# Late attention tiles on one Trainium2 core: pairing a tile's scores with the values' product of its second last tile

## The chip, the cores and the metric

The kernel runs as one program on one core of a Trainium2 chip. The metric is device time in microseconds (us), median of several runs. One more execution was recorded by the profiler; all rows below come from it.

## The reference

```python
# attention in chunks of 32 queries; context: 16 keys left, 8 right, and 8 memory keys
scores = scale * np.matmul(q_c, k_full.transpose(0, 1, 3, 2))
scores = scores - np.max(scores, axis=-1, keepdims=True)
a = np.exp(scores)
a = a / (np.sum(a, axis=-1, keepdims=True) + 1e-09)
out[:, :, c_start:c_end] = np.matmul(a, v_full)      # (4, 8, 768, 64)
...
gate = 1.0 / (1.0 + np.exp(-(x @ w_gate)))           # x: 3072 x 512, d_ff 1536
x = (gate * (x @ w_val)) @ w_out
h = x @ w_in                                         # d_ff 2048
out = (h * (1.0 / (1.0 + np.exp(-1.702 * h)))) @ w_out
```

## The kernel before

The 3072 tokens are 32 attention tiles of 96 tokens, and 6 blocks of 512 tokens for the two gated networks. Each operand of a network's product is split into a high and a low part, so that a product is three matrix products.

**Early and late tiles.** Nine tiles are done early: TensorE transposes for them. The other 23, the late tiles (numbered 0 to 22 here, in the order of their work), run between the products of the first network's blocks. Block b's products (`first_product`, L771 and L778, then the gate, L795 to L806, then `gemm2`, L962) share the engines with the attention tiles of block b+1. A late tile goes through these steps:

- SyncE (SP) loads queries, keys, memory keys and values by many small DMAs, all through one helper (L323): 12 for the queries, 16 to 20 for the keys of two tiles, 2 or 3 for the values. SP issues one after the other. Queries have two buffers (`f`), keys two (`raw`), values one (`vn`).
- VectorE (DVE) turns queries (`ev_q`, L498, into `qt`) and keys (`ev_k`, L506, into `kt`) in 32 x 32 blocks. `qt` and `kt` have one buffer each.
- TensorE (PE) makes the scores (`pe_s`, L521), in the two PSUM banks that are `bank_70` and `bank_71`.
- DVE takes the maximum (L538), subtracts it (L541); ScalarE (ACT) takes exp (L549); DVE sums (L578), adds 1e-9 and inverts (L580, L581).
- The norm (L589) multiplies by the inverse, into `pn` (the buffer is `raw_78` in the rows): 56 key columns of all 96 rows on GpSimd (POOL), and the 8 memory columns on DVE, in two instructions of 64 and 32 rows.
- DVE turns the result (`ev_pt`, L643, eight instructions, into `pt`, one buffer).
- PE multiplies with the values (`pe_pv`, L668), in the same two banks.
- ACT and DVE evict the banks to `xh` and `xl` (L713, L716). Tokens of the last two blocks go another way: ACT evicts to `qt` (L691), and SP stores `qt` to `x_dram` by L323. The next `ev_q` writes `qt` and has to wait for that store. Of the late tiles, 7 to 10 and 16 to 22 have such tokens.

**Bursts.** On PE a late tile's scores are one burst with the values' product of the tile before it: first `pe_pv` of tile n-1, then `pe_s` of tile n. So between two bursts a tile goes through its whole chain, from the maximum to `pt`.

**Other work in these stretches.** `park` (L996) adds the two parts of 24 weights on GpSimd into two staging buffers, and SP stores them to `wf_dram` by L323; a third park waits for the first one's store.

**The order** is made by a list scheduler (`Schedule`): every step is added with an engine, a planned duration, what it reads and writes, and for products a due time. A step's due time is the earliest of its followers', less its duration, a latency and a slack. Each engine takes, of its steps that are ready in planned time, the one due first. The order is fixed when the program is built: each engine works through its list in that order, and waits where an input is not there. A DMA costs 0.45 us of SP in the plan:

```python
add("sp", 0.45, lambda: nc.sync.dma_start(out=dst(), in_=src), r=list(r), w=[key], nbytes=n)
```

Of the kernel before, what the change touches and what calls it, by code (L numbers as in the profile page):

```python
# [123 lines left out]
def c_dve(n, k=1):  # L124
    return k * 0.13 + n / 960.0
# [11 lines left out]
def kernel(  # L137
# [221 lines left out]
    def attention(t, bufs, banks, pe_path, extra=None, last=False):  # L359
# [6 lines left out]
        kk = bufs.k  # L366
        T = bufs.t

        def tadd(eng, dur, fn, r=(), w=(), **kw):
            add(eng, dur, fn, r=r, w=w, slack=SL, **kw)  # L370

        def load_ctx(name, src, mem):

# [60 lines left out]
        else:  # L434
# [78 lines left out]
            tadd("dve", c_dve(2 * 384), ev_k, r=kkb, w=[(kk["kt"], 0), (kk["kt"], 1)])  # L513
# [42 lines left out]
        if pe_path:  # L556
            tadd("pe", 0.75, pe_s, r=rs, w=[kb0, kb1], margin=mg)
        else:

            held = late.pop() if late else None  # L560

            def pe_burst():
                if held:
                    held[0]()
                pe_s()

            tadd("pe", 1.6, pe_burst, r=rs + (held[1] if held else []), w=[kb0, kb1])
            if held:
                held[2]()
            load_ctx("vn", v, mem_v)  # L570
        for hp, kb in enumerate((kb0, kb1)):
            tadd("dve", 0.34 + edge, lambda hp=hp: ev_max(hp), r=[kb], w=[(kk["mx"], hp)])
        for hp, kb in enumerate((kb0, kb1)):
            tadd("dve", 0.34, lambda hp=hp: ev_sub(hp), r=[kb, (kk["mx"], hp)], w=[(kk["e"], hp)])
        ke = [(kk["e"], 0), (kk["e"], 1)]
        tadd("act", c_act(512), ev_exp, w=ke)
        tadd(
# [15 lines left out]
        if pe_path:  # L593

            def ev_norm(c):
                r = (c * CH, (c + 1) * CH)
                eng = nc.vector if en[c] == "dve" else nc.gpsimd
                norm(eng, T["pw"][r[0] : r[1], :, c * CH : c * CH + CTX], r, (0, CTX))

            def ev_norm_m():  # L600
                norm(nc.vector if en[0] == "dve" else nc.gpsimd, T["pw"][:, :, TK:P], (0, TQ), (CTX, KW))

            en = ["pool", "pool", "pool"] if t in (0, 2) else ["dve", "pool", "pool"]
            for c in range(NCK):
                tadd(en[c], 0.75 if en[c] == "dve" else 1.2, lambda c=c: ev_norm(c), r=ke + [kk["sm"]], w=[(kk["pw"], c)])
            tadd(en[0], 0.25 if en[0] == "dve" else 0.35, ev_norm_m, r=ke + [kk["sm"]], w=[(kk["pw"], 3)])

            def pe_pt():
                for h in range(H):
                    a, p = divmod(h, NP)  # L610
                    nc.tensor.transpose(
                        bt[a][:, p * TQ : (p + 1) * TQ], T["pw"][:, h, :], ident()[:TQ, :TQ]
                    )

            def ev_pt(a):
                src = bt[a][:, : NP * TQ]
                dst = T["pt"].rearrange("p (a h) s -> p a (h s)", a=2)[:, a, :]
                nc.scalar.activation(dst, src, AF.Copy)

            tadd("pe", 0.7, pe_pt, r=[(kk["pw"], c) for c in range(4)] + [bufs.kid], w=kbt, margin=mg)  # L620
            for a in range(2):
                tadd("act", c_act(384), lambda a=a: ev_pt(a), r=[kbt[a]], w=[(kk["pt"], a)])
        else:

            def ev_norm():
                norm(nc.vector, T["pn"][0:L, :, 3 * CH - NM : 3 * CH], (0, L), (CTX, KW))
                norm(nc.vector, T["pn"][L:TQ, :, CTX:KW], (L, TQ), (CTX, KW))

            tadd(
                "pool",  # L630
                0.95,
                lambda: norm(nc.gpsimd, T["pn"][:, :, 0:CTX], (0, TQ), (0, CTX)),
                r=ke + [kk["sm"]],
                w=[(kk["pn"], 0)],
            )
            tadd("dve", c_dve(128, 2), ev_norm, r=ke + [kk["sm"]], w=[(kk["pn"], 1)])
# [87 lines left out]
        if pe_path:  # L724
            tadd("pe", 0.8, pe_pv, r=rp, w=[kbv], margin=mg)
            if t < NPRO - 1 or t >= NPRO:
                evict()
            else:

                evict(0)  # L730
                held_back.append(lambda: evict(1))
        else:
            late.append((pe_pv, rp, evict))
            if last:
                tadd("pe", 0.9, pe_pv, r=rp, w=[kb0, kb1])
# [440 lines left out]
    def x_prep(b, mark=None, src=y_dram, b0=0, rk=lambda m, bb: [("y", m, bb)]):  # L1176
        for k in range(2):
            tk = 4 + k
            for i, (m, bb) in enumerate(((k, b), (k, b + 1), (2 + k, b), (2 + k, b + 1))):

                def load(i=i, m=m, bb=bb):
                    c = slice((bb - b0) * BLK, (bb - b0 + 1) * BLK)
                    nc.sync.dma_start(out=ys[i], in_=src[m * P : (m + 1) * P, c])

                add("sp", 0.45, load, r=rk(m, bb) + ([mark] if mark else []), w=[KYS[i]], nbytes=P * BLK * 4)

            def sub(o, x, y):
                def fn():
# [363 lines left out]
```

## Time and profile before

| | us |
|---|---|
| median of 3 runs | 1183.88 |
| lowest, highest | 1183.59, 1184.81 |
| profiled execution, its own time | 1182.71 |
| its span, first to last instruction | 1180.7 |

In the profile an engine's busy time counts its instructions on data; instructions that issue a DMA or wait for a semaphore are not counted. `[4.71 <-DMA f<-in_q_dram]` behind a row says that the engine was idle for 4.71 us ahead of it, and that the landing of a DMA from `in_q_dram` to `f` ended that. PE stands idle for few microseconds of its span; it slows down where its clock is granted at the lower of two levels (1.2 instead of 2.4 GHz).

### The profile page before, as it was taken

Reading aid. Unit: us, or ns where it says so; the run is one execution under the profiler, and the core shown is the slowest. Engines: PE = TensorE matmul, PEld = TensorE weight load, DVE = VectorE, ACT = ScalarE, POOL = GpSimd, SP = SyncE. Lnnn points to the kernel's source line nnn. Section 1 sums busy time; section 2 is a strip of 40 time slices with the busy share of each in tenths; the row PEclk is TensorE's granted clock in tenths of the full one; section 3 lists DMA queues with packets and bytes.
Section 4 is the critical chain, followed back from the end, with each engine's and each line's share of the span. In section 5 each row is a group of like instructions: output and inputs, shape, how many; then the busy total and the mean of one; then the engine's idle time right before and its main releaser. Section 6 shows DMA issues by size and latency. Waiting matters only on the chain.

```text
span 1180.7 us, 19478 instructions
## 1 busy us (share of the span) xinstructions
PE 1152.8 (98%) x7288; PEld 961.2 (81%) x7288; DVE 797.8 (68%) x1506; ACT 529.9 (45%) x953; POOL 114.5 (10%) x104
## 2 busy tenths in 40 slices
PE   8899999999989999999999999999999999999998
PEld 7788898997778788888888888888888888888887
DVE  7899668887878567888786978878343356243442
ACT  6778522223212222476554767755233344243332
POOL 5333313011122000000000000000000000000000
PEclk9899999999999999999999999999999999999999
DMA  9766244335344421533436555675243443244100
GB/s 210 221 186 187 74 108 106 55 60 130 67 89 102 98 55 38 174 117 108 150 118 227 181 164 182 205 219 160 67 123 105 121 149 115 63 127 125 35 36 36
DMA packets 211069, 144.39 MB, mean 122 GB/s; under 512 B 146208, under 2 KB 166944, under 8 KB 210976
## 3 DMA queue, kind: packets, MB, share of 16 engines
q1 hardware_dynamic: 207520, 136.87, 41.5%
q10 hardware_dynamic: 3456, 6.29, 1.4%
q8 instruction: 57, 0.93, 0.3%
q14 instruction: 36, 0.29, 0.1%
HBM read 107.45 MB, written 35.65 MB: 121 GB/s over the span
## 4 chain that ended last, share of the span: by engine, by line
PE 82%; SPq 6%; DVE 5%; DMA 3%; issue 2%; ACT 1%; POOL 0%; DVEq 0%; ACTq 0%; POOLq 0%
PE bank L1306 29%; PE bank L745 22%; PE bank L962 13%; PE bank L771 10%; SPq L323 6%; PE bank L778 5%; DVE pt L643 1%; PE bank L668 1%; PE bank L521 1%; DVE raw L589 1%; DMA y_dram<-f 1%; DMA wf_dram<-f 1%; DMA raw<-in_moe_w_out_dram 1%; DVE pw L589 0%; DVE sm L578 0%
## 5 line engine op out<-in xcount | busy, mean ns | idle before, releaser
L1306 PE MATMUL bank<-sb_x,sb_r 128*128 128x512 f32 x1512 | 362.8, 389 | 0.7 <-ACT sb_s L1318 0.7
L1306 PEld LDWEIGHTS bank<-sb_x,sb_r 128*128 128x128 f32 x1512 | 283.6, 188 | 60.6 <-ACT sb_s L1318 1.8
L745 PE MATMUL bank<-w,gh 128*128 128x512 f32 x624 | 192.0, 389 | 0.0
L771 PE MATMUL bank<-xh,w 128*128 128x512 f32 (+1 forms) x464 | 161.2, 359 | 5.0 <-DVE sig L798 3.0
L771 PE MATMUL bank<-xl,w 128*128 128x512 f32 (+1 forms) x464 | 159.6, 355 | 0.0
L962 PE MATMUL bank<-gh,w 128*128 128x512 f32 (+1 forms) x656 | 157.3, 364 | 1.0 <-ACT f L982 1.0
L745 PEld LDWEIGHTS bank<-w,gh 128*128 128x128 f32 x624 | 117.1, 188 | 24.3
L962 PEld LDWEIGHTS bank<-gh,w 128*128 128x128 f32 x656 | 114.8, 189 | 21.3 <-ACT f L982 1.4
L1322 DVE TENSOR_TENSOR sb_s<-bank,sb_s 128x512 f32<-128x512 f32 x108 | 74.3, 690 | 73.7 <-PE bank L1306 61.8
L745 PE MATMUL bank<-w,gl 128*128 128x512 f32 x312 | 121.4, 389 | 0.0
L778 PE MATMUL bank<-xh,w 128*128 128x512 f32 (+1 forms) x464 | 109.0, 359 | 0.0
L1318 ACT ACTIVATE sb_s<-bank 128x512 f32<-128x512 f32 x108 | 65.1, 603 | 87.9 <-PE bank L1306 82.0
L771 PEld LDWEIGHTS bank<-xh,w 128*128 128x128 f32 x464 | 88.7, 191 | 19.4 <-DVE sig L798 3.8
L771 PEld LDWEIGHTS bank<-xl,w 128*128 128x128 f32 x464 | 88.7, 191 | 12.3
L778 PEld LDWEIGHTS bank<-xh,w 128*128 128x128 f32 x464 | 78.4, 190 | 12.9 <-issue 0.2
L803 ACT ACTIVATE gh<-sig 128x512 fp32r<-128x512 f32 (+1 forms) x58 | 32.3, 557 | 110.1 <-DVE sig L798 109.7
L643 DVE STREAM_TRANSPOSE pt<-raw 32x256 f32<-32x256 f32 x184 | 79.9, 434 | 2.3
L962 PE MATMUL bank<-gl,w 128*128 128x512 f32 (+1 forms) x328 | 80.3, 367 | 1.1 <-DVE gl L806 1.1
L1349 ACT ACTIVATE sig<-sb_s 128x512 f32<-128x512 f32 x72 | 45.3, 632 | 57.0 <-DVE sb_s L1322 36.0
L745 PEld LDWEIGHTS bank<-w,gl 128*128 128x128 f32 x312 | 58.6, 188 | 12.3
L795 ACT ACTIVATE sig<-bank 128x512 f32<-128x512 f32 (+1 forms) x58 | 30.6, 528 | 83.7 <-PE bank L778 74.7
L962 PEld LDWEIGHTS bank<-gl,w 128*128 128x128 f32 x328 | 56.8, 189 | 10.8 <-DVE gl L806 1.3
(162 smaller groups left out, 1480.9 us busy)
## 6 DMA issues: line engine op xcount, KB each, us to landing
sb_r<-wc_dram SPq DMA_DIRECT2D x133, 256.0 KB
raw<-in_moe_w_out_dram SPq DMA_DIRECT2D x24, 512.0 KB
raw<-in_moe_w_in_dram SPq DMA_DIRECT2D x16, 512.0 KB
wc_dram<-sb_r SPq DMA_DIRECT2D x15, 512.0 KB
wf_dram<-f SPq DMA_DIRECT2D x24, 256.0 KB
y_dram<-f ACTq DMA_DIRECT2D x24, 256.0 KB
raw<-wf_dram SPq DMA_DIRECT2D x24, 256.0 KB
out_dram<-f SPq DMA_DIRECT2D x23, 256.0 KB
```

The lines of the kernel that those rows point to most:

```text
L323: add("sp", 0.45, lambda: nc.sync.dma_start(out=dst(), in_=src), r=list(r), w=[key], nbytes=n)
L643: nc.vector.transpose(T["pt"][r * CH : (r + 1) * CH, :, c * CH : (c + 1) * CH], T["pn"][c * CH : (c + 1) * CH, :, kb * CH : (kb + 1) * CH],)
L745: nc.tensor.matmul(ps_out, a, c, start=(first and i == 0 and j == 0), stop=(last and i == n - 1 and j == 2),)
L771: nc.tensor.matmul(bank[bk][:, :n], w[:, 0, ts[t]], x[xb][:, t, c0 : c0 + n], start=t == 0 and x is xhs, stop=False)
L778: nc.tensor.matmul(bank[bk][:, :n], w[:, 1, ts[t]], xhs[xb][:, t, c0 : c0 + n], start=False, stop=t == NK - 1)
L795: nc.scalar.activation(sig[:, :n], bank[src_sig][:, :n], AF.Tanh, scale=scale / 2)
L803: nc.scalar.activation(gh[:, :n], sig[:, :n], AF.Copy, scale=0.5)
L962: nc.tensor.matmul(bank[into[m]][:, c0 : c0 + n], w[:, wi, m * P : (m + 1) * P], g[:, :n], start=f == 0 and j == 0 and c0 == 0, stop=f == ...
L1306: nc.tensor.matmul(bank[bk], w[:, o : o + P], xt[x, k][:, xl, :], start=first and k == 0 and wl == 0 and xl == 0, stop=k == 1 and wl == 1, ...
L1318: add("act", c_act(BLK), lambda: nc.scalar.activation(work[n], bank[bk], AF.Copy), r=[("bank", bk)], w=[n])
L1322: nc.vector.tensor_tensor(out=work[n], in0=bank[bk], in1=work[n], op=ALU.add)
L1349: add("act", c_act(BLK), lambda: nc.scalar.activation(sigs[i], src(), AF.Tanh, scale=0.851), r=[ksrc], w=[ks])
```

## The change

It touches the late tiles and numbers of the scheduler.

1. A burst pairs the scores of tile n with the values' product of tile n-2 (before: n-1). The list `late` holds two tiles; a tile's second half (`rest`: loading the values, norm, `ev_pt`) is added to the schedule after the burst of the next tile, since `vn`, `pn` and `pt` have one buffer each. After the last tile two tiles are finished one after the other.
2. GpSimd forms all norms: the two instructions for the memory columns move there from DVE.
3. Planned durations: `ev_k` 0.97 (before 0.93), maximum and subtraction 0.42 each (before 0.34), `ev_pt` 1.75 for each half (before 1.59), a burst 1.75 or 0.8 (before 1.6), and 13.3 ns (before 2.5 ns) on each product from block 1 on. A burst is due 4 us sooner, the first loads of `x_prep` 10 us sooner. SP's 0.45 us stays.

```diff
-            held = late.pop() if late else None
+            held = late.pop(0) if len(late) > 1 else None
...
                 if held:
-                    held[0]()
+                    held["pv"]()
                 pe_s()
-            tadd("pe", 1.6, pe_burst, r=rs + (held[1] if held else []), w=[kb0, kb1])
+            tadd("pe", 1.75 if held else 0.8, pe_burst, r=rs + (held["rp"] if held else []), w=[kb0, kb1], more=4.0)
             if held:
-                held[2]()
-            load_ctx("vn", v, mem_v)
+                held["evict"]()
+            for x in late:
+                x["rest"]()
+        d_sm = 0.34 if pe_path else 0.42
...
             def ev_norm():
-                norm(nc.vector, T["pn"][0:L, :, 3 * CH - NM : 3 * CH], (0, L), (CTX, KW))
-                norm(nc.vector, T["pn"][L:TQ, :, CTX:KW], (L, TQ), (CTX, KW))
+                norm(nc.gpsimd, T["pn"][0:L, :, 3 * CH - NM : 3 * CH], (0, L), (CTX, KW))
+                norm(nc.gpsimd, T["pn"][L:TQ, :, CTX:KW], (L, TQ), (CTX, KW))
...
+            def rest():
+                load_ctx("vn", v, mem_v)
                 tadd(
-                    "dve",
-                    c_dve(1024, 4),
-                    lambda part=part: ev_pt(part),
-                    r=[(kk["pn"], 0), (kk["pn"], 1)],
-                    w=[(kk["pt"], part)],
+                    "pool",
+                    0.95,
+                    lambda: norm(nc.gpsimd, T["pn"][:, :, 0:CTX], (0, TQ), (0, CTX)),
...
+                tadd("pool", 0.6, ev_norm, r=ke + [kk["sm"]], w=[(kk["pn"], 1)])
...
-            late.append((pe_pv, rp, evict))
+            late.append(dict(pv=pe_pv, rp=rp, evict=evict, rest=rest))
             if last:
-                tadd("pe", 0.9, pe_pv, r=rp, w=[kb0, kb1])
-                late.pop()[2]()
+                for x in list(late):
+                    if x is not late[0]:
+                        x["rest"]()
+                    tadd("pe", 0.9, x["pv"], r=x["rp"], w=[kb0, kb1])
+                    x["evict"]()
...
     for b in range(NB - 2):
         n = BLK
+        if b:
+            step_ns[0] = 32 / 2400.0
```

**SP, before: from the store of tile 16's last tokens to that of tile 17's.** The order counts SP's DMAs; the first row here is the 503rd from the first late tile's first query load on, the last one the 551st. `f_79` and `f_80` are the two query buffers, `raw_77` one of the two for keys.

```order
L323 DMA x_dram<-qt 128x4x64
L323 DMA f_79<-in_mem_k_dram 8x4x32 x4
L323 DMA f_79<-in_q_dram 32x4x32 x3
L323 DMA wf_dram<-f_82 128x512
L323 DMA f_79<-in_q_dram 32x4x32 x9
L323 DMA f_80<-in_q_dram 32x4x32 x12
L323 DMA raw_77<-in_k_dram 32x7x32 x16
L323 DMA vn<-in_v_dram 112x8x64
L323 DMA vn<-in_mem_v_dram 8x8x64
L323 DMA x_dram<-qt 128x4x96
```

**SP, with the change: the same two stores.** They are now the 526th and the 564th.

```order
L323 DMA x_dram<-qt 128x4x64
L323 DMA f_80<-in_q_dram 32x4x32 x5
L323 DMA raw_77<-in_k_dram 32x7x32 x12
L323 DMA wf_dram<-f_82 128x512
L323 DMA raw_77<-in_k_dram 32x7x32 x4
L323 DMA f_79<-in_q_dram 32x4x32 x12
L323 DMA vn<-in_v_dram 112x8x64
L323 DMA vn<-in_mem_v_dram 8x8x64
L323 DMA vn<-in_v_dram 8x8x64
L323 DMA x_dram<-qt 128x4x96
```

The loads of a tile's queries stand further ahead of these stores than before: with the change the queries of tile 21 come ahead of the second store, before they come behind it. Tile 17's store comes after burst 19 with the change (before: burst 18), and `ev_q` of tile 20 waits for it (before: of tile 19).

On PE, ahead of the scores of tile 20 with the change stand 1024 product instructions of 512 columns and 720 of 256; ahead of the scores of tile 18 before stand 1020 and 720. So the bursts of tile 18 before and of tile 20 with the change stand at the same place among the products, four instructions apart.

**DVE, before: from the maximum of tile 16 to the end of its `ev_pt`** (`xl` is the eviction, `sig` and `gl` the network's gate, `qt` and `kt` the next tile's).

```order
L538 TENSOR_REDUCE mx<-bank_70 96x4
L538 TENSOR_REDUCE mx<-bank_71 96x4
L541 TENSOR_TENSOR e<-bank_70,mx 96x256
L541 TENSOR_TENSOR e<-bank_71,mx 96x256
L506 STREAM_TRANSPOSE kt<-raw_77 128x768
L498 STREAM_TRANSPOSE qt<-f_79 128x384
L578 TENSOR_REDUCE sm<-e 96x8
...
L581 RECIPROCAL sm<-sm 96x8
L589 TENSOR_TENSOR raw_78<-e,sm 64x8x8
L589 TENSOR_TENSOR raw_78<-e,sm 32x8x8
L798 SCALAR_TENSOR_TENSOR sig_84<-sig_84,bank_69 128x512
L643 STREAM_TRANSPOSE pt<-raw_78 32x8x32 x8
```

**DVE, with the change: from the maximum of tile 15 to the end of its `ev_pt`** (L580, L583 and L635 are now the lines of sum, inverse and `ev_pt`).

```order
L538 TENSOR_REDUCE mx<-bank_70 96x4
L538 TENSOR_REDUCE mx<-bank_71 96x4
L498 STREAM_TRANSPOSE qt<-f_80 128x384
L541 TENSOR_TENSOR e<-bank_70,mx 96x256
L541 TENSOR_TENSOR e<-bank_71,mx 96x256
...
L580 TENSOR_REDUCE sm<-e 96x8
...
L583 RECIPROCAL sm<-sm 96x8
L811 SCALAR_TENSOR_TENSOR gl_88<-sig_84,gh_86 128x512
L506 STREAM_TRANSPOSE kt<-raw_77 128x768
L635 STREAM_TRANSPOSE pt<-raw_78 32x8x32 x8
```

The two norms are gone from DVE. `ev_q` of the next tile stands right behind the maximum, ahead of the subtractions, the gate and everything else of the stretch. And `ev_pt` of tile 15 now runs behind burst 16, which still reads `pt` of tile 14.

## Rows read from the trace of the kernel before

**Rows 1.** The page, part 1: busy us, share of the span, instructions.

```profile
span 1180.7 us, 19478 instructions
PE 1152.8 (98%) x7288; PEld 961.2 (81%) x7288; DVE 797.8 (68%) x1506; ACT 529.9 (45%) x953; POOL 114.5 (10%) x104
```

**Rows 2.** Waits of PE, whole span: total us, times, longest.

```profile
PE bank L668 <- DVE pt L643: 8.7, 5, 3.7
PE bank L771 <- DVE sig L798: 3.0, 3, 1.5
```

**Rows 3.** Chain of waits in 150 to 490 us, by line.

```profile
by line: SPq L323 21.0%; PE bank L771 20.4%; PE bank L962 15.3%; PE bank L778 11.0%; issue 4.9%; DVE pt L643 4.8%; PE bank L668 3.9%; PE bank L521 3.0%; DVE raw L589 2.9%; DMA y_dram<-f 2.4%; DMA wf_dram<-f 2.0%; DMA raw<-in_k_dram 1.5%; AC
```

**Rows 4.** SP's timeline: start, length, what, how many DMAs.

```profile
135.17 0.80 SPq L323 DMA_DIRECT2D f<-in_q_dram  x2
...
324.01 1.48 SPq L323 DMA_DIRECT2D f<-in_q_dram  x3
...
326.88 5.67 SPq L323 DMA_DIRECT2D f<-in_q_dram  x12
...
396.01 0.39 SPq L323 DMA_DIRECT2D x_dram<-qt  x1
396.44 1.43 SPq L323 DMA_DIRECT2D f<-in_mem_k_dram  x4
```

**Rows 5.** Busy time of each engine in 138 to 411 us.

```profile
138.00:411.00 273.00, 258.65 (x2487) 224.22 (x2486) 206.47 (x456) 70.08 (x165) 50.09 (x44) 0.99 0.40 88
```

**Rows 6.** SP's own waits in 138 to 411 us.

```profile
SPq L323 <- DMA y_dram<-f: 4.3, 4, 1.8
SPq L323 <- PE bank L778: 1.8, 2, 1.6
SPq L323 <- DMA raw<-in_k_dram: 0.7, 1, 0.7
```

**Rows 7.** DVE's timeline ahead of burst 13.

```profile
327.45 0.58 DVE L498 STREAM_TRANSPOSE qt<-f 128x384 f32<-128x384 f32 x1 [4.71 <-DMA f<-in_q_dram]
...
328.26 3.58 DVE L589 TENSOR_TENSOR raw<-e,sm 64x64 f32<-64x64 f32 x2
...
332.14 3.57 DVE L643 STREAM_TRANSPOSE pt<-raw 32x256 f32<-32x256 f32 x8
```

**Rows 8.** PE's timeline at burst 13.

```profile
335.77 0.88 PE L668 MATMUL bank<-pt,vn 128*64 128x96 f32 x16 [3.72 <-DVE pt L643]
...
337.36 2.07 PE L778 MATMUL bank<-xh,w 128*128 128x512 f32 x4
```

**Rows 9.** DVE's timeline ahead of burst 18.

```profile
398.99 0.58 DVE L498 STREAM_TRANSPOSE qt<-f 128x384 f32<-128x384 f32 x1 [4.91 <-DMA f<-in_mem_k_dram]
...
404.72 0.69 DVE L798 SCALAR_TENSOR_TENSOR sig<-sig,bank 128x512 f32<-128x512 f32 x1
```

**Rows 10.** PE's timeline at burst 18.

```profile
405.46 0.50 PE L771 MATMUL bank<-xh,w 128*128 128x512 f32 x1 [1.54 <-DVE sig L798]
...
415.52 1.07 PE L778 MATMUL bank<-xh,w 128*128 128x512 f32 x4
416.43 1.07 PE L962 MATMUL bank<-gl,w 128*128 128x512 f32 x4
417.43 0.88 PE L668 MATMUL bank<-pt,vn 128*64 128x96 f32 x16
418.24 0.74 PE L521 MATMUL bank<-kt,qt 64*32 64x64 f32 x48
418.91 0.50 PE L962 MATMUL bank<-gh,w 128*128 128x512 f32 x1
```

**Rows 11.** DVE's groups by form, 150 to 490 us: busy us, mean ns, idle before.

```profile
L589 DVE TENSOR_TENSOR raw<-e,sm 32x64 f32<-32x64 f32 x23 | 27.8, 1209 | 0.3
...
L541 DVE TENSOR_TENSOR e<-bank,mx 96x256 f32<-96x256 f32 x46 | 17.4, 411 | 2.2 <-ACT qt L691 1.8
L806 DVE SCALAR_TENSOR_TENSOR gl<-sig,gh 128x512 fp32r<-128x512 f32 x24 | 17.3, 722 | 7.1 <-ACT gh L803 7.0
...
L589 DVE TENSOR_TENSOR raw<-e,sm 64x64 f32<-64x64 f32 x23 | 7.3, 318 | 0.6
```

**Rows 12.** POOL's groups by form, whole span.

```profile
L996 POOL TENSOR_TENSOR f<-w 128x512 f32<-128x512 f32 x24 | 31.1, 1306 | 45.0 <-DMA wf_dram<-f 32.1 <-ACT sig L795 11.7 <-DMA y_dram<-f 1.2
...
L589 POOL TENSOR_TENSOR raw<-e,sm 96x448 f32<-96x448 f32 x23 | 21.9, 952 | 234.4 <-DVE sm L581 233.4 <-ACT kt L510 0.9
...
L589 POOL TENSOR_TENSOR pw<-e,sm 96x64 f32<-96x64 f32 x2 | 0.9, 452 | 0.2
```

More of the change, by code (lines that the diff above doesn't have):

```diff
@@ L367, in attention, with tadd @@
         T = bufs.t
-        def tadd(eng, dur, fn, r=(), w=(), **kw):
-            add(eng, dur, fn, r=r, w=w, slack=SL, **kw)
+        def tadd(eng, dur, fn, r=(), w=(), more=0.0, **kw):
+            add(eng, dur, fn, r=r, w=w, slack=SL + more, **kw)
         def load_ctx(name, src, mem):
@@ L512, in attention @@
             tadd("dve", c_dve(384), ev_q, r=kqb, w=[kk["qt"]])
-            tadd("dve", c_dve(2 * 384), ev_k, r=kkb, w=[(kk["kt"], 0), (kk["kt"], 1)])
+            tadd("dve", 0.97, ev_k, r=kkb, w=[(kk["kt"], 0), (kk["kt"], 1)])
             tadd("act", c_act(NP * NCK * NM), ev_m, r=[kk["mt"]], w=[(kk["kt"], 0), (kk["kt"], 1)])
@@ L558, in attention @@
         else:
-            held = late.pop() if late else None
+            held = late.pop(0) if len(late) > 1 else None
             def pe_burst():
                 if held:
-                    held[0]()
+                    held["pv"]()
                 pe_s()
-            tadd("pe", 1.6, pe_burst, r=rs + (held[1] if held else []), w=[kb0, kb1])
+            tadd("pe", 1.75 if held else 0.8, pe_burst, r=rs + (held["rp"] if held else []), w=[kb0, kb1], more=4.0)
             if held:
-                held[2]()
-            load_ctx("vn", v, mem_v)
+                held["evict"]()
+            for x in late:
+                x["rest"]()
+        d_sm = 0.34 if pe_path else 0.42
         for hp, kb in enumerate((kb0, kb1)):
-            tadd("dve", 0.34 + edge, lambda hp=hp: ev_max(hp), r=[kb], w=[(kk["mx"], hp)])
+            tadd("dve", d_sm + edge, lambda hp=hp: ev_max(hp), r=[kb], w=[(kk["mx"], hp)])
         for hp, kb in enumerate((kb0, kb1)):
-            tadd("dve", 0.34, lambda hp=hp: ev_sub(hp), r=[kb, (kk["mx"], hp)], w=[(kk["e"], hp)])
+            tadd("dve", d_sm, lambda hp=hp: ev_sub(hp), r=[kb, (kk["mx"], hp)], w=[(kk["e"], hp)])
         ke = [(kk["e"], 0), (kk["e"], 1)]
@@ L625, in ev_norm @@
             def ev_norm():
-                norm(nc.vector, T["pn"][0:L, :, 3 * CH - NM : 3 * CH], (0, L), (CTX, KW))
-                norm(nc.vector, T["pn"][L:TQ, :, CTX:KW], (L, TQ), (CTX, KW))
[L629 to L636, printed above, removed]
+                norm(nc.gpsimd, T["pn"][0:L, :, 3 * CH - NM : 3 * CH], (0, L), (CTX, KW))
+                norm(nc.gpsimd, T["pn"][L:TQ, :, CTX:KW], (L, TQ), (CTX, KW))
             PTB = ((0, 0, 0), (1, 0, 1), (2, 0, 2), (0, 1, 1), (1, 1, 2), (2, 1, 3), (0, 2, 3), (1, 2, 3))
@@ L646, in ev_pt @@
                     )
-            for part in range(2):
+            def rest():
+                load_ctx("vn", v, mem_v)
                 tadd(
-                    "dve",
-                    c_dve(1024, 4),
-                    lambda part=part: ev_pt(part),
-                    r=[(kk["pn"], 0), (kk["pn"], 1)],
-                    w=[(kk["pt"], part)],
-                )
+                    "pool",
+                    0.95,
+                    lambda: norm(nc.gpsimd, T["pn"][:, :, 0:CTX], (0, TQ), (0, CTX)),
+                    r=ke + [kk["sm"]],
+                    w=[(kk["pn"], 0)],
+                )
+                tadd("pool", 0.6, ev_norm, r=ke + [kk["sm"]], w=[(kk["pn"], 1)])
+                for part in range(2):
+                    tadd(
+                        "dve",
+                        1.75,
+                        lambda part=part: ev_pt(part),
+                        r=[(kk["pn"], 0), (kk["pn"], 1)],
+                        w=[(kk["pt"], part)],
+                    )
         if pe_path:
@@ L732, in attention @@
         else:
-            late.append((pe_pv, rp, evict))
+            late.append(dict(pv=pe_pv, rp=rp, evict=evict, rest=rest))
             if last:
-                tadd("pe", 0.9, pe_pv, r=rp, w=[kb0, kb1])
-                late.pop()[2]()
+                for x in list(late):
[3 more added lines that the diff above has]
+                    x["evict"]()
+                late.clear()
     def mm3(ps_out, lhs, rhs, first, last):
@@ L1174, in split_x, with x_prep @@
         add("pool" if pool else "dve", c_pool(BLK) if pool else c_dve(BLK), lo, r=[kst], w=[("X", m, k)])
-    def x_prep(b, mark=None, src=y_dram, b0=0, rk=lambda m, bb: [("y", m, bb)]):
+    def x_prep(b, mark=None, src=y_dram, b0=0, rk=lambda m, bb: [("y", m, bb)], slack=0.0):
         for k in range(2):
@@ L1183, in load @@
                     nc.sync.dma_start(out=ys[i], in_=src[m * P : (m + 1) * P, c])
-                add("sp", 0.45, load, r=rk(m, bb) + ([mark] if mark else []), w=[KYS[i]], nbytes=P * BLK * 4)
+                add("sp", 0.45, load, r=rk(m, bb) + ([mark] if mark else []), w=[KYS[i]], nbytes=P * BLK * 4, slack=slack)
             def sub(o, x, y):
@@ L1405 @@
     produce1(1)
-    x_prep(NB - 2, None, x_dram, NB - 2, lambda m, bb: [("xd", bb, t) for t in in_block(bb)])
+    x_prep(NB - 2, None, x_dram, NB - 2, lambda m, bb: [("xd", bb, t) for t in in_block(bb)], 10.0)
     ngh[0] = last1[2] + 1
```

## The prediction

> **What bounds the kernel now.** I read the page's busy times first [rows 1]: PE works in 98% of the span, so only two things can be won: moments in which PE stands, and its speed. For the moments I took the waits of PE [rows 2]: 8.7 us in five waits of the values' product for `ev_pt`, and 3.0 us for the gate (`sig`). Both lie in the stretch of the late tiles. There the chain of waits [rows 3] names as its largest owner not PE and not DVE but SP's queue: 21.0% for L323, the one line through which all small DMAs pass; `ev_pt` has 4.8%, the norm 2.9%.
>
> So I turned to SP's timeline [rows 4]. From the first late query load at 135.17 to the store of tile 16's last tokens at 396.01, its 503rd DMA, SP issues 502 DMAs in 260.84 us: 0.520 us each, where the plan has 0.45. Twelve query loads in a row take 5.67 us, 0.47 each. Waiting explains little of it: in 138 to 411 us SP waits 4.3 + 1.8 + 0.7 = 6.8 us [rows 6]. Without these, (260.84 - 6.8) / 502 = 0.506 each; without the waits for `y_dram` alone, 0.511. SP is busy all through, 0.06 to 0.07 us an issue behind its plan, and never catches up. In the same stretch the 16 DMA engines are busy at 0.40 [rows 5]: the issue limits, not the moving of bytes.
>
> Two stalls show how SP reaches PE. Ahead of burst 13 SP issues the last of tile 13's queries at 324.01, for 1.48 us; `ev_q` starts at 327.45 after DVE stood 4.71 us for that landing; then come the norms (3.58 us) and `ev_pt` (3.57 us), all late [rows 7], and PE stands 3.72 us. After that its first four product matmuls take 2.07 us instead of 1.07 [rows 8, 10]. Ahead of burst 18 it is the store: DMA 503 starts at 396.01, and `ev_q` of tile 18, which writes the buffer that this store reads, starts at 398.99, 2.98 us later. (The row puts the wait down to `in_mem_k`, but those four loads are issued only from 396.44 on and fill the other query buffer, which this `ev_q` doesn't read; the store is what fits the order.) Behind `ev_q` the gate's `sig` runs at 404.72, and a product waits 1.54 us for it [rows 9, 10].
>
> **The change, part by part.** *Norms.* DVE loses 46 instructions, 27.8 + 7.3 = 35.1 us [rows 11]. The one of 32 rows takes 1.209 us and the one of 64 rows 0.318, so most of that is time in which it was held up. DVE was busy for 206.47 of 273 us, 76% [rows 5], and goes to about 63%. GpSimd gets them at no more than 0.452 us each, the row of the nearest shape (96x64): up to 20.8 us, on 50.09 of 273 [rows 5, 12]. Neither engine is full, so this pays only where `ev_pt` ends a PE wait: at most the 8.7 us. The cover has a hole: GpSimd works in order, and its `park` stood 32.1 us for SP's stores to `wf_dram` [rows 12]; a norm queued behind such a `park` is late when SP is late.
>
> *Pairing.* The chain from maximum to `ev_pt` gets two tiles' time instead of one, so the five waits should go: up to -8.7 us, with the gate's waits -11.7, and PE's whole idle time in 138 to 411 us, 273 - 258.65 = 14.35 us, is the most that can be won. The values' product of a tile, its eviction and its store move one burst back. For tiles 16 to 22 that matters, since `ev_q` of tile n+3 now waits for the store of tile n, where tile n+2 did.
>
> *Planned durations.* Products get 13.3 ns instead of 2.5, bursts and DVE's steps get longer, SP's 0.45 stays. In planned time the products take longer while SP is as quick as before. So between the same two products more DMAs are put on SP's list. This is the term that I take as decisive, and the order gives its size. Burst 20 with the change stands at the product at which burst 18 stood, four 512-column matmuls further on. Burst 18 needed DMA 503 to be through; burst 20 needs DMA 564 (the store of tile 17): 61 more.
>
> *When burst 20 can run.* At f us an issue DMA 564 starts at 135.17 + 563 f. Then 2.98 us to `ev_q` as at burst 18 [rows 9], `ev_q` itself 0.58, and two subtractions at 0.411 [rows 11], which now stand behind it and which free the banks: 4.38 us together.
>
> - f = 0.506 (no waits): 420.0 + 4.4 = 424.4
> - f = 0.511: 422.9 + 4.4 = 427.3
> - f = 0.520 (as measured, waits and all): 427.7 + 4.4 = 432.1
>
> *When PE could run it.* Burst 18 began at 417.43 [rows 10]. Add four matmuls (a group of four takes 1.07, less its overlap 1.00 from start to start: 416.43 to 417.43, so about 0.9 to 1.0), two more score groups at 418.91 - 418.24 = 0.67, and one more values' product at 418.24 - 417.43 = 0.81: 420.5. If all stalls ahead of it went, PE would be there up to 14.35 us sooner, but it would only wait there for longer: burst 20 is set by SP.
>
> The lateness is thus 3.9, 6.8 or 11.6 us. I take f = 0.515, between the last two, since the waits for `wf_dram`, keys and products come with work that stays, while the waits for `y_dram` may shift: 425.1 + 4.4 = 429.5, 9.0 us late. What follows burst 20 is unchanged PE work, so the end moves by the same: 1182.71 + 9.0 = 1191.7 on the scale of the profiled execution. The median lies 1.17 above that execution (1183.88 - 1182.71): **1193 us**.
>
> Costed at nothing: the later end of the attention. After burst 22 two tiles must still be finished, one more than before, and the last two blocks' products need their tokens; a values' product is 0.88 us on PE [rows 8] and is hidden as long as products of other blocks remain. The `x_prep` loads that are due 10 us sooner are the same number of DMAs; ahead of DMA 564 they are already counted in the 61.
>
> A rule speaks against all this. The Trainium skill, "DMA: Bandwidth & Descriptors", section "Issuing engines are not separate DMA queues", says that spreading DMAs over engines saves only the issuing sequencer's time, which is usually small relative to the DMA itself; its section "Anatomy of one DMA" puts a sequencer's dispatch at about 50 ns (for DMAs that GpSimd issues). By that price 61 issues are an estimated 3 us, burst 20 would have its queries long before PE gets there, and the change would end as in rival A. This trace disagrees for these DMAs of SP: 0.47 to 0.52 us each, back to back, with the DMA engines at 0.40 [rows 4, 5].
>
> **The rivals.**
>
> *A, faster: SP is not the pace.* The issue time could stretch because there is time, each DMA waiting for room that a later one would not need. For it: `ev_pt` does end the largest PE waits [rows 2]; against it: SP's list has hardly a gap, and both stalls above start from it [rows 4, 7, 9]. Then PE keeps the 8.7 us and perhaps the gate's 3.0: 1183.9 - 8.7 = 1175, and between 1169.5 (all 14.35) and 1181 (a quarter of the waits). It decides if DMA 564 starts by 420.5 - 4.4 = 416.1, that is at (416.1 - 135.17) / 563 = 0.499 us an issue or less.
>
> *B, about the same: SP runs with no waits*, f from 0.499 to 0.506: 0 to 3.9 us late, 1184 to 1188, less what is won behind burst 20. For it: the plan with longer products may spread the waits; against it: products and loads that SP waits for are all still there.
>
> *C, worse than forecast: late queries hold up the gate.* `ev_q` now stands right behind the maximum, ahead of subtractions, `sig` and `gl`. If it waits for SP, the network's products wait too, not only the burst. Burst 18 showed such a wait of 1.54 us when `sig` came 5 us behind `ev_q` [rows 9, 10]. Each longer stop of PE also costs speed: after the one of 3.72 us the first four matmuls took 2.07 instead of 1.07, 1.0 us lost in that group [rows 8, 10]. Three or four such places at 2 us each, or a norm held behind a `park`, add 6 to 8 us: 1198 to 1201.
>
> *D, the waits for `ev_pt` do not go*, because it now waits for the burst behind it to have read `pt`. It then runs right after the burst and has a whole tile for 3.57 us [rows 7]; I give this no time of its own.
>
> **How the numbers follow.** The forecast (SP sets burst 20, 1187 to 1197) gets 0.56, A 0.18, B 0.13, C 0.13. The range 1178 to 1200 takes in both bounds of f, all of B, the upper third of A and most of C, and leaves out some 0.12 of A and 0.06 of C. The forecast's own range is 1187 to 1197. A measurement of this kernel can tell about 0.2%, 2.4 us, from no change: 1181.5 to 1186.3. B lies mostly there: same 0.12. Slower: the forecast, C and a little of B, 0.70. Faster: A, 0.18.
>
> **What would show it.** Right: SP issues without gaps until about 425 to 430, DMA 564 starts near 425; DVE stands ahead of `ev_q` of tile 20, ended by a DMA; PE has one long stop ahead of burst 20, near 420 to 430, and low-clock matmuls behind it; the waits for `ev_pt` are gone and no norm is on DVE, whose busy time falls by some 35 us. Wrong at the issue rate: DMA 564 starts before 416, no stop at burst 20 (A, B). Wrong at the place: stops ahead of `sig` products at tiles 9 to 13 or 17 already (C). The forecast is wrong as a whole if PE's waits shrink by more than SP's lateness adds, which needs 0.499 us an issue.

## The result, and the profile after

The changed kernel takes 1195.59 us (median of 4 runs, 1194.64 to 1196.35) against 1184.35 of before (4 runs, three of which had given the 1183.88): the ratio is 1.0094, 95% interval 1.0077 to 1.0112. It is slower by 11.2 us; the forecast was 1193, with 1178 to 1200 as its range. The profiled execution took 1196.35 us, with a span of 1194.6.

The page, part 1, of the changed kernel (busy us, share of the span, instructions):

```profile
span 1194.6 us, 19493 instructions
PE 1156.5 (97%) x7288; PEld 963.7 (81%) x7288; DVE 771.1 (65%) x1460; ACT 530.4 (44%) x953; POOL 129.5 (11%) x150
```

Beside [rows 1]: DVE lost 26.7 us of work, POOL gained 15.0, and PE is busy 3.7 us longer with the same 7288 matmuls. The span grew by 13.9. Where the rest lies is shown by the view of windows, first with a row of before, then with two of the changed kernel (window; length; busy of PE, PEld, DVE, ACT, POOL; granted clock; DMA share; GB/s):

```profile
138.00:500.00 362.00, 347.65 (x3173) 296.61 (x3172) 271.99 (x595) 97.66 (x223) 54.76 (x49) 1.00 0.38 89
```

```profile
138.00:411.00 273.00, 250.59 (x2481) 217.91 (x2480) 181.13 (x422) 66.20 (x159) 61.95 (x80) 0.97 0.38 82
...
138.00:500.00 362.00, 337.94 (x3111) 287.94 (x3110) 241.56 (x549) 96.08 (x221) 70.43 (x95) 0.98 0.39 89
```

The first row of the changed kernel answers to [rows 5]: the clock in 138 to 411 us is 0.97 and was 0.99. In 138 to 500 us PE stood for 362 - 347.65 = 14.35 us before and 24.06 us with the change: 9.7 us more. With the 3.7 us of slower matmuls (clock 0.98 against 1.00) that is 13.4 of the 13.9. The waits of PE in that stretch with the change (total us, times, longest):

```profile
PE bank L669 <- DMA vn<-in_mem_v_dram: 11.1, 6, 3.4
PE bank L776 <- DVE sig L803: 6.6, 3, 5.8
PE bank L669 <- DVE sm L580: 2.5, 1, 2.5
PE bank L776 <- ACT sig L800: 1.4, 2, 0.9
PE bank L669 <- DMA vn<-in_v_dram: 1.1, 1, 1.1
```

The waits for `ev_pt`, 8.7 us in [rows 2], are gone. In their place stand 12.2 us for loads of values, and 6.6 us for `sig` (3.0 before). The 2.5 us that a row puts down to the sum (`sm`) belong to the values too, as is shown below, which makes 14.7 us for them. So the further idle time adds up: 14.7 for values and 3.6 more for `sig`, less 8.7 for `ev_pt`, is 9.6 us. The chain of waits in 150 to 490 us, by line, begins:

```profile
by line: SPq L323 42.0%; PE bank L776 15.0%; PE bank L967 11.6%; PE bank L783 7.0%; issue 6.1%; DVE pt L635 4.1%; PE bank L669 2.1%; DMA raw<-in_k_dram 1.9%; DMA f<-in_q_dram 1.6%; PE bank L521 1.6%; DMA y_dram<-f 1.4%; DVE kt L506 0.9%; DV
```

SP's small DMAs have gone from 21.0% [rows 3] to 42.0%. SP's timeline with the change (start, length, what, count):

```profile
134.15 0.80 SPq L323 DMA_DIRECT2D f<-in_q_dram  x2
...
223.94 1.85 SPq L323 DMA_DIRECT2D f<-in_q_dram  x4
225.84 7.45 SPq L323 DMA_DIRECT2D raw<-in_k_dram  x12
233.69 0.33 SPq L323 DMA_DIRECT2D vn<-in_v_dram  x1
234.08 0.44 SPq L323 DMA_DIRECT2D vn<-in_mem_v_dram  x1
...
291.44 1.80 SPq L323 DMA_DIRECT2D f<-in_mem_k_dram  x4
...
385.27 0.39 SPq L323 DMA_DIRECT2D vn<-in_v_dram  x1
385.70 0.45 SPq L323 DMA_DIRECT2D vn<-in_mem_v_dram  x1
...
429.64 0.39 SPq L323 DMA_DIRECT2D x_dram<-qt  x1
```

PE's timeline, at three of its stops and at burst 20:

```profile
236.96 0.88 PE L669 MATMUL bank<-pt,vn 128*64 128x96 f32 x16 [3.43 <-DMA vn<-in_mem_v_dram]
...
302.03 0.80 PE L776 MATMUL bank<-xh,w 128*128 128x512 f32 x1 [5.76 <-DVE sig L803]
...
388.43 1.44 PE L669 MATMUL bank<-pt,vn 128*64 128x96 f32 x16 [2.53 <-DVE sm L580]
...
434.75 0.88 PE L669 MATMUL bank<-pt,vn 128*64 128x96 f32 x16
```

And DVE's timeline ahead of the last three:

```profile
295.13 0.31 DVE L478 STREAM_TRANSPOSE f<-f 128x128 f32<-128x128 f32 x1 [4.25 <-DMA f<-in_mem_k_dram]
...
296.61 3.54 DVE L635 STREAM_TRANSPOSE pt<-raw 32x256 f32<-32x256 f32 x8
...
301.29 0.69 DVE L803 SCALAR_TENSOR_TENSOR sig<-sig,bank 128x512 f32<-128x512 f32 x1
...
381.11 3.58 DVE L635 STREAM_TRANSPOSE pt<-raw 32x256 f32<-32x256 f32 x8 [3.48 <-POOL raw L591]
...
432.11 0.58 DVE L498 STREAM_TRANSPOSE qt<-f 128x384 f32<-128x384 f32 x1 [2.19 <-DMA x_dram<-qt]
432.61 0.71 DVE L541 TENSOR_TENSOR e<-bank,mx 96x256 f32<-96x256 f32 x2
```

Two kinds of stop can be read here, and a delay that is hidden behind one of them; all three begin at SP. **Values:** `vn` was free from 224.04, when the values' product before had ended; its load went out at 233.69, since SP had sixteen query and key loads ahead of it; PE waited 3.43 us at 236.96. **Gate:** at 295.13 DVE had stood 4.25 us for memory keys that SP issued from 291.44 on; `kt`, 3.54 us of `ev_pt` and the maximum followed, and only then `sig` at 301.29, for which PE waited 5.76 us. **Norm:** at 381.11 `ev_pt` came 3.48 us late for GpSimd's norm, and `xl`, which frees the banks for the next burst, ended only at 387.25. PE stood until 388.43 all the same, but not for the sum that its row names: that sum itself ends at 388.43. By the semaphores in the packed trace PE's weight load was waiting for the two loads of values that SP had sent out at 385.27 and 385.70, and these landed at 388.19 and 388.30. So this is one more stop for values, with the norm's delay behind it. GpSimd's timeline shows where that delay comes from, and its groups by form how much there is of it:

```profile
377.64 2.55 POOL L1001 TENSOR_TENSOR f<-w 128x512 f32<-128x512 f32 x2 [14.10 <-DMA wf_dram<-f]
380.14 1.55 POOL L591 TENSOR_TENSOR raw<-e,sm 96x448 f32<-96x448 f32 x3
```

```profile
L1001 POOL TENSOR_TENSOR f<-w 128x512 f32<-128x512 f32 x24 | 31.4, 1317 | 100.3 <-DMA wf_dram<-f 67.5 <-DMA y_dram<-f 25.1 <-DVE sm L583 7.3
...
L591 POOL TENSOR_TENSOR raw<-e,sm 64x64 f32<-64x64 f32 x23 | 7.9, 345 | 0.0
L591 POOL TENSOR_TENSOR raw<-e,sm 32x64 f32<-32x64 f32 x23 | 7.8, 338 | 1.7
```

`park` stood 67.5 us for SP's stores (32.1 in [rows 12]), with norms queued behind it. The small norms themselves are cheap there: 0.345 and 0.338 us.

### The profile page after: what moved, and what is told of

Its sections match the earlier page's. It is cut to its first block, busy times and chain, and to the rows that moved or that the text cites. A ratio compares the mean times of both kernels' runs of the same rounds, so it can differ in the third digit from the quotient of the medians.

```text
span 1194.6 us, 19493 instructions
## 1 busy us (share of the span) xinstructions
PE 1156.5 (97%) x7288; PEld 963.7 (81%) x7288; DVE 771.1 (65%) x1460; ACT 530.4 (44%) x953; POOL 129.5 (11%) x150
## 4 chain that ended last, share of the span: by engine, by line
PE 79%; SPq 12%; DVE 4%; DMA 2%; issue 2%; ACT 1%; POOL 0%; DVEq 0%; ACTq 0%; POOLq 0%
PE bank L1313 29%; PE bank L750 22%; PE bank L967 12%; SPq L323 12%; PE bank L776 9%; PE bank L783 5%; DVE pt L635 1%; PE bank L669 1%; PE bank L521 1%; DMA raw<-in_k_dram 1%; DVE pw L591 0%; DVE mx L538 0%; DMA f<-in_q_dram 0%; DMA y_dram<-f 0%; DVE sm L580 0%
## 5 line engine op out<-in xcount | busy, mean ns | idle before, releaser
L635 DVE STREAM_TRANSPOSE pt<-raw 32x256 f32<-32x256 f32 x184 | 79.7, 433 | 10.5 <-POOL raw L591 5.0
L750 PEld LDWEIGHTS bank<-w,gl 128*128 128x128 f32 x312 | 58.6, 188 | 12.2
L301 POOL TENSOR_TENSOR w<-f,w 128x512 fp32r<-128x512 f32 x17 | 27.1, 1591 | 370.1 <-ACT w L296 370.0
```

The costliest lines, as they stand in the source:

```text
L301: eng.tensor_tensor(out=w[:, 1, :], in0=ft, in1=w[:, 0, :].bitcast(F32), op=ALU.subtract)
L635: nc.vector.transpose(T["pt"][r * CH : (r + 1) * CH, :, c * CH : (c + 1) * CH], T["pn"][c * CH : (c + 1) * CH, :, kb * CH : (kb + 1) * CH],)
L750: nc.tensor.matmul(ps_out, a, c, start=(first and i == 0 and j == 0), stop=(last and i == n - 1 and j == 2),)
```

## The experiments

Every ratio is to the kernel before, timed on the same chip; idle time of PE is for 138 to 500 us.

**Values from ScalarE's queue** (the changed kernel):

```diff
-        add("sp", 0.45, lambda: nc.sync.dma_start(out=dst(), in_=src), r=list(r), w=[key], nbytes=n)
+        add("sp", 0.45, lambda: by.dma_start(out=dst(), in_=src), r=list(r), w=[key], nbytes=n)
...
-                dma(lambda a=a, z=z: T[name][a:z], s.rearrange("h s d -> s h d"), ks[-1], r=pre)
+                dma(lambda a=a, z=z: T[name][a:z], s.rearrange("h s d -> s h d"), ks[-1], r=pre, by=nc.sync if pe_path else nc.scalar)
```

> The changed kernel, every instruction in the place that it had, but the late tiles' loads of values go out on ScalarE's queue in place of SP's (51 of the late tiles' 598 DMAs leave SP's list; the store of tile 17 becomes SP's DMA 522 instead of 564). Theory (SP's issue is what the late tiles wait for): SP is up to 20 us ahead at that store, PE's waits for the values (12.2 us in 138 to 500 us of the changed kernel) go, the 5.8 us stop for sig goes too, PE's idle time in the stretch falls from 24.1 us to 8 or less, and the time to 1176 to 1184. Rival 1 (the values wait because they have one buffer and a load takes its time to land): the waits stay about as they are, 1193 to 1197. Rival 2 (only the values were late, the rest of SP's lateness costs nothing): the value waits go, the others stay, 1183 to 1186.

1189.5 us, 1.0048 (1.0031 to 1.0065); PE idle 18.1 us. The waits for values are gone (0.2 us are left) and 6 us of the 11.2 are back, so the stop was not the landing of a load into a single buffer. But the stop for the gate (4.7 us) stayed, and the norm's delay, with no late values to hide it, now stopped PE for 6.2 us. GpSimd's timeline ahead of that stop, with the `park` in front of the norms:

```profile
369.37 2.53 POOL L1001 TENSOR_TENSOR f<-w 128x512 f32<-128x512 f32 x2 [15.56 <-DMA wf_dram<-f]
371.86 1.55 POOL L591 TENSOR_TENSOR raw<-e,sm 96x448 f32<-96x448 f32 x3
```

No account fits in full: the time lies in none of the three ranges. The theory's waits shrank, but less than it said, and SP was relieved less than it assumed: tile 17's store goes out at 422.04, 7.6 us sooner and not 20. SP's waits in 138 to 430 us say why:

```profile
SPq L323 <- DMA vn<-in_v_dram: 15.6, 10, 4.3
```

In the packed trace the DMAs of SP and of ScalarE take turns at eight semaphores, and a DMA is sent out only when the one that had its semaphore before it has landed. 14.2 of these 15.6 us are such waits of an SP DMA for values which ScalarE had sent for late. For example, SP's key load of 272.21 waited for values that ScalarE sent for at 268.85 and that landed at 272.19.

**The plan's price of a small DMA, 0.52 in place of 0.45** (the changed kernel):

```diff
-        add("sp", 0.45, lambda: nc.sync.dma_start(out=dst(), in_=src), r=list(r), w=[key], nbytes=n)
+        add("sp", 0.52, lambda: nc.sync.dma_start(out=dst(), in_=src), r=list(r), w=[key], nbytes=n)
```

> The changed kernel, with 0.52 us in place of 0.45 us as the plan's price of one of SP's small DMAs; nothing else. The store of tile 17 becomes DMA 531 (was 564) and burst 20 stands at about the same products. Theory (the plan asks SP for more than it can do): 135.17 + 530 x 0.515 + 4.4 = 412.5, before PE is there, so no lateness is left; 1174 to 1184. Rival (SP's total rate is the limit whatever the order): 1190 to 1196.

1179.87 us, 0.9961 (0.9948 to 0.9974): 15.7 us below the changed kernel, and faster than before. PE stands for 362 - 350.85 = 11.15 us:

```profile
138.00:500.00 362.00, 350.85 (x3180) 298.89 (x3178) 256.38 (x574) 104.30 (x234) 69.45 (x95) 0.99 0.40 93
```

Its waits of PE:

```profile
PE bank L669 <- DVE xl L717: 3.1, 2, 1.9
PE bank L669 <- DMA raw<-in_k_dram: 3.0, 1, 3.0
PE bank L776 <- DVE sig L803: 1.4, 1, 1.4
PE bank L669 <- DMA vn<-in_mem_v_dram: 1.0, 1, 1.0
```

SP issues as fast as in the changed kernel, DMA 531 at 412.95, (412.95 - 134.04) / 530 = 0.526 us each. Only the order is another, and the waits for values fall from 14.7 to 1.0 us. The 3.0 us put down to a key load are no wait for keys, which that product doesn't read: by the semaphores they ended when DVE's `xl` freed a bank.

**Pairing undone** (the changed kernel; `rest()` is called at once):

```diff
-            held = late.pop(0) if len(late) > 1 else None
+            held = late.pop(0) if late else None
...
```

> The changed kernel with the pairing undone: a burst takes the values' product of the tile just before it, and norm and values are added right behind the sums; durations, slack and GpSimd's norms stay. In the order burst 18 stands some 55 us of products later than burst 18 of the changed kernel. Theory (pairing is what lets the bursts run ahead of SP; the planned durations alone don't): SP's lateness is gone, PE waits for pt come back in part, 1176 to 1186. Rival (the longer planned products push DMAs ahead of the same product, with or without pairing): 1190 to 1196.

1227.57 us, 1.037 (1.0355 to 1.0385), outside both. It doesn't tell the theories apart, because the order of the nine early tiles changed as well. The waits of PE over the whole span begin:

```profile
PE bank L611 <- POOL pw_a L589: 17.9, 2, 10.9
PE bank L773 <- DVE sig L800: 12.4, 4, 7.5
```

The two stops of these 17.9 us end at 87.61 and 116.22 us, ahead of any late tile. In 138 to 500 us PE stood for 13.0 us, and its waits there name no load.

**2.5 ns on each product again** (the changed kernel):

```diff
-        if b:
-            step_ns[0] = 32 / 2400.0
```

> The changed kernel with 2.5 ns instead of 13.3 ns planned on each product of blocks 1 to 3; all else stays. The store of tile 17 becomes DMA 544 (was 564), and burst 20 stands about 4 us of products sooner. By the sum of the prediction burst 20 is 135.17 + 543 x 0.515 + 4.4 = 419.2 against about 414: 5.5 us late, 1187 to 1190. If the 13.3 ns are the whole cause, as the prediction has it: 1183 or less. If they have no part in it: 1194 to 1197.

1187.15 us, 1.0029 (1.0016 to 1.0042); PE idle 15.4 us. That is the figure which the sum gives (1187 to 1190), with DMA 544 at 417.16 where the sum has 414.8. But the stop of 5.5 us that the sum puts at burst 20 isn't there: the longest after 400 us is 1.7 us. PE's waits name no load of values any more. So the longer planned products cost 8.4 us of the 11.2. They are a large part of the loss, not all of it.

**The norms on GpSimd, in the kernel before:**

```diff
-                norm(nc.vector, T["pn"][0:L, :, 3 * CH - NM : 3 * CH], (0, L), (CTX, KW))
+                norm(nc.gpsimd, T["pn"][0:L, :, 3 * CH - NM : 3 * CH], (0, L), (CTX, KW))
...
-            tadd("dve", c_dve(128, 2), ev_norm, r=ke + [kk["sm"]], w=[(kk["pn"], 1)])
+            tadd("pool", 0.6, ev_norm, r=ke + [kk["sm"]], w=[(kk["pn"], 1)])
```

> The kernel before, with its two small norms of each late tile on GpSimd and planned there (0.6 us), as in the change; nothing else. In the order the store of tile 16 is SP's DMA 509 (before: 503) and burst 18 stands where it stood. Theory (SP sets the pace, DVE's relief is worth at most the five waits for pt, 8.7 us): 1179 to 1186. Rival 1 (DVE's load is what makes the late tiles late): all five waits and the gate's go, 1176 or less. Rival 2 (norms queued on GpSimd behind a park that waits for SP's store are late, and pt with them): 1188 or more.

1183.98 us, 0.9986 (0.9967 to 1.0004): no difference that can be told. DVE's busy time in the stretch fell from 271.99 to 233.92 us, and PE still stood for 13.9.

**The norms on DVE, in the changed kernel** (the same lines the other way).

> The changed kernel with the two small norms on DVE again, planned there as before; SP's list stays the same (tile 17's store is DMA 564). Theory (SP sets the time of the late tiles): within 3 us of the changed kernel, 1193 to 1199. Rival 1 (the norms on GpSimd, behind parks, cost the time): 1190 or less. Rival 2 (DVE is short of time): 1201 or more, by some of the 35 us that these norms took on DVE before.

1194.48 us, 1.0088 (1.0071 to 1.0105), PE idle 23.0 us: as the changed kernel. DVE is busy for 274.59 us there, 33 more than in the changed kernel, at no cost. So DVE's load was not what bound the late tiles, in either kernel.

**Pairing alone, with the planned numbers of before:**

```diff
-            held = late.pop() if late else None
+            held = late.pop(0) if len(late) > 1 else None
...
```

One number of the change stayed in this kernel: the first loads of `x_prep` are due 10 us sooner.

> The kernel before with the pairing alone: planned durations, slack, due times and the norms' engine as before. Tile 17's store becomes DMA 536, and burst 20 stands some 9 us of products later than in the changed kernel. Theory (pairing brings the bursts nearer to their loads and costs part of the loss; the longer planned products the rest): SP is late in places, 1185 to 1191. Rival 1 (pairing is a gain when SP keeps up with the plan, and only the 13.3 ns put SP behind): 1182 or less. Rival 2 (pairing is the whole loss): 1193 or more.

1200.24 us, 1.0138 (1.0122 to 1.0155): the second rival. Pairing loses more alone than with the other numbers, and mostly not at SP: PE's waits name no load, and 15.7 us go to waits of the burst put down to `xl`. DVE's timeline ahead of one of them, of 5.6 us, in which the burst started at 271.60:

```profile
261.39 3.38 DVE L591 TENSOR_TENSOR raw<-e,sm 32x64 f32<-32x64 f32 x1
264.81 0.98 DVE L506 STREAM_TRANSPOSE kt<-raw 128x768 f32<-128x768 f32 x1
265.71 3.54 DVE L635 STREAM_TRANSPOSE pt<-raw 32x256 f32<-32x256 f32 x8
269.28 0.75 DVE L538 TENSOR_REDUCE mx<-bank 96x4 f32<-96x256 f32 x2
...
270.57 0.71 DVE L541 TENSOR_TENSOR e<-bank,mx 96x256 f32<-96x256 f32 x2
271.21 0.60 DVE L717 TENSOR_TENSOR xl<-bank,xh 128x192 fp32r<-128x192 f32 x2
```

And GpSimd's, beside that norm:

```profile
262.17 2.53 POOL L1001 TENSOR_TENSOR f<-w 128x512 f32<-128x512 f32 x2
```

The scores of this tile were ready from about 261. Behind a small norm (3.38 us), `kt` and `ev_pt` its maximum and its subtraction came only at 269.28 and 270.57, and `xl` at 271.21; these read the two banks which the next burst writes. So in this order it is the banks, held by a late DVE, that stop PE. Pairing alone with the norms on GpSimd was not tried.

**A quarter of the query loads from ScalarE's queue** (the changed kernel; 3 of 12 loads a tile):

```diff
-                            r=pre,
+                            r=pre, by=nc.scalar if r == 0 else nc.sync,
```

> The changed kernel, every instruction in its place, but of the 12 query loads of a late tile the 3 for the first 32 partitions go out on ScalarE's queue instead of SP's. SP has a tenth to a sixth fewer DMAs; tile 17's store is its DMA 478 instead of 564, at 135 + 477 x 0.522 = 384 if nothing else holds it. Theory (SP's issue is the pace): the waits of PE for values, sig and pt shrink to half or less of 24 us, 1174 to 1185. Rival (ScalarE, which issues in order as well, is held up by these loads and passes that on to exp and sig): 1188 or more, with ScalarE's waits for the query buffers in the trace.

1185.4 us, 1.0012 (1.0002 to 1.0021), 10 us below the changed kernel; PE idle 16.9 us, so down by 30%, not by half. The time stands 0.4 us above what the theory gave. With every other instruction in its place, relief of SP gives most of the loss back. SP is relieved less than expected here too. (The expectation's DMA 478 counts from a later first load; from the same place in the list tile 17's store is DMA 498, which at 0.525 us would go out at 394.7 and not at 384.) It goes out at 418.09. SP's waits in 138 to 430 us begin:

```profile
SPq L323 <- DMA f<-in_q_dram: 24.0, 17, 2.3
```

These are the waits of e1 again: 20.2 of the 24.0 us pass at SP DMAs whose semaphore a query load of ScalarE's had before. ScalarE sends these loads out between its other work.

**0.52 in the kernel before** (the one number of e2).

> The kernel before with 0.52 us in place of 0.45 as the plan's price of one of SP's small DMAs; nothing else. The store of tile 16 becomes DMA 475 (was 503), about 15 us sooner at 0.52 an issue, so the stops ahead of bursts 13 and 18 that came from late loads shrink. If the price alone is the gain of the changed kernel with 0.52 (1179.9) and pairing has none: 1178 to 1181. If pairing and the other numbers bring something of their own once SP keeps up: 1182 to 1185, slower than 1179.9 by 2 us or more.

1189.6 us, 1.0039 (1.0020 to 1.0058): slower than before, which neither account had. No wait of PE in the stretch names a load, and SP waits 17.9 us for values' products that free `vn`, so it is ahead. PE's waits begin:

```profile
PE bank L668 <- DVE pt L643: 11.7, 5, 4.7
```

The waits for `ev_pt`, 8.7 us in [rows 2], have grown. With loads in time, the chain from maximum to `ev_pt` within one tile is what stops PE. The whole change at the same price has 1179.87, without such waits: at 0.52 the change is worth 9.7 us, at 0.45 it costs 11.2.

**0.52 with pairing alone.**

> Pairing alone (1200.2) with 0.52 as the plan's price of a small DMA. Tile 17's store becomes DMA 532 (was 536 there), hardly sooner, though earlier stores move up by 15 to 24 places. Theory (SP's lateness makes the loss of pairing alone): 1180 to 1190. Rival (pairing alone loses by uneven bursts, whatever SP's price, since its steps' planned durations are too short): 1195 or more.

1194.0 us, 1.0080 (1.0057 to 1.0103), in neither range, nearer to the rival: 6.2 us below pairing alone, PE idle 23.1 us. SP is not held to the pace here: DMA 532 at 432.1 is 0.564 us an issue.

**0.56 and 0.38 in the changed kernel** (the one number of e2).

> The changed kernel with 0.56 us as the plan's price of a small DMA. The order has the same stores within one DMA of that with 0.52 and bursts 1 to 7 us of products later between tiles 9 and 15. Theory (what counts is that the plan doesn't ask for more than SP's real 0.52): 1177 to 1181, as with 0.52. Rival (each hundredth of planned price moves work away from SP and gains on): 1176 or less.

> The changed kernel with 0.38 us as the plan's price of a small DMA, further from the real 0.52 than the 0.45 that it has. Tile 17's store stays DMA 564, tile 16's goes from 526 to 542, those of tiles 7 to 10 come 26 to 33 places later. Theory (a too low price makes PE wait for SP, at many places): slower than the changed kernel by 2 to 8 us, 1198 to 1204, with more waits for values and late ev_q. Rival (only the store of tile 17 at burst 20 counts, as the prediction has it): 1194 to 1197.

0.56: 1189.28 us, 1.0039 (1.0025 to 1.0053), slower than 0.52, against both accounts. 0.38: 1204.63 us, 1.0170 (1.0147 to 1.0193), as the theory has it, which went slightly beyond its range. Waits of PE with 0.38:

```profile
PE bank L669 <- DMA vn<-in_mem_v_dram: 14.0, 3, 7.7
PE bank L776 <- DVE sig L803: 6.0, 2, 5.5
PE bank L669 <- DMA vn<-in_v_dram: 4.4, 2, 4.1
```

And with 0.56:

```profile
PE bank L967 <- ACT gh L808: 5.9, 3, 2.0
PE bank L669 <- DVE xl L717: 5.1, 3, 2.8
```

| price in the plan | median us | PE idle us | of it for loads of values | real us per issue up to tile 17's store |
|---|---|---|---|---|
| 0.38 | 1204.63 | 29.2 | 18.4 | 0.534 |
| 0.45 (the change) | 1195.59 | 24.1 | 14.7 | 0.525 |
| 0.52 | 1179.87 | 11.2 | 1.0 | 0.526 |
| 0.56 | 1189.28 | 15.8 | 0 | 0.544 |

The part for loads falls with the price all the way; it is the other waits, for the gate and the banks, that grow again at 0.56. Why that order has them was read only from its rows, and stays open.

## Why the prediction was right, and which of its steps were not

**SP is the pace: shown.** SP's price in the plan alone, from 0.38 to 0.52, moves the time by 24.8 us and the waits for values from 18.4 to 1.0. Taking DMAs off SP without moving anything else gives back 6 (e1) and 10 us (e8), though SP then stood 15.6 and 24.0 us for landings. The rate forecast was 0.515 us; DMA 564 started at 429.64, (429.64 - 134.15) / 563 = 0.525, against 425.1.

**The sum's size was right, its place wrong, and that the figure came so near is in part luck.** `ev_q` of tile 20 began at 432.11, behind the landing of the store, as forecast (2.47 us after the store went out; 2.98 was taken). The subtractions ended at 433.3, and burst 20 started at 434.75, 14.2 us later than the 420.5 of the sum and 5.2 later than the 429.5 forecast. But PE made no stop there. It had lost the time before, in a string of smaller stops, of which three are shown above. The step that failed is "burst 20 is set by SP" as the one place: SP's lateness reaches PE at many places, whichever load is next. Price 0.38 shows it as well: tile 17's store is SP's DMA 564 there too, and the time is 9.0 us longer. The one stop of 9.0 us that the sum forecast, and the 14.7 + 3.6 - 8.7 us of waits and 3.7 us of clock that were measured, have only SP in common.

**A term was missing.** Among the things that PE and DVE wait for, the sum has queries and stores and leaves out the values. Their loads go out behind whole groups of queries and keys, mostly 7 to 10 us after `vn` is free (224.04 to 233.69 in the rows above), and cost 14.7 us, more than any other wait.

**Rival C was part of the truth.** The stop of 5.76 us at 302.03 is its mechanism (late data at the head of DVE's list hold the gate), though memory keys and not queries were late, and the hole named under the norms, `park` ahead of a norm, held `ev_pt` by 3.48 us; a stop of PE came of it in e1, 6.2 us long, while the changed kernel's stop at 388.43 ended with the values. The slower clock cost 3.7 us of busy time.

**That the planned durations are the decisive term was half right.** Undoing the 13.3 ns gives 8.4 us back (e4), near the sum for that order. But pairing alone, without them, loses 15.8 us, and by another cause: banks that a late DVE holds (e7). The other new durations and slack, with the norms, repair 13.1 us of that loss (e4 against e7); which of them does it was not tried. The 13.3 ns then add SP's lateness.

**The norms were costed at nothing, rightly** (e5, e6), and the five waits for `ev_pt` did go, against rival D. DVE's busy time fell by 26.7 and not 35 us. **Rival A fell**: no gain from DVE's relief, and SP never came near 0.499 us an issue. Nor does the issue stretch with the time that there is: SP's instruction for a query load takes 0.43 us at the median before, with the change, and in e1, e2 and e8. The Trainium skill, "DMA: Bandwidth & Descriptors", section "Issuing engines are not separate DMA queues", calls the time to initiate a DMA usually small relative to the DMA itself. Against one load the trace agrees: PE starts 2.88 us after the values of 234.08 were sent for. But 564 of them stand in one list, 0.525 us apart, and there the small part decides the time.

## What to carry to other kernels

A list scheduler that is given longer, truer durations for some engines and keeps a too low one for the queue that feeds them can make things worse: here it put more loads ahead of the same product than the queue could bring. Read the queue's real time per issue from the trace (here 0.52 us against 0.45 in the plan) and correct it together with the rest; the same change then wins 0.39% instead of losing 0.94%. But don't take such a number as a knob with one direction: 0.56 was worse than 0.52, and 0.52 alone made the kernel before slower, since each order shifts the stop to the next resource.

## What the runs showed of the hardware

SP's time per small DMA hardly moves, 0.52 to 0.53 us, in before, the change, e2, e4, e5, e6 and e12, however the orders differ. In e1, e3 and e7 to e11 it is longer, 0.54 to 0.57, since SP waits more there. DMAs sent out by ScalarE can hold SP up through the semaphores that both use, for 14.2 us in e1 and 20.2 in e8. And an instruction beside another engine's can take many times its own time: the small norm of 32 rows took 3.38 us on DVE in e7, ending 0.07 us after two `park` instructions on GpSimd, where the one of 64 rows took 0.318 us on average before [rows 11] and the same norm takes 0.338 us on GpSimd.
